# Nine weight blocks split straight out of PSUM, layer two's sums grown in their banks, and a new order of the steps

## Chip, cores and metric

The kernel runs on one core of one Trainium2 chip. The metric is the device time of one execution in microseconds (us), as the median of several runs. Engines are named as the profile names them: PE is TensorE (matmuls; PEld its weight loads), DVE is VectorE, ACT is ScalarE, POOL is GpSimd, SP is SyncE, which issues the DMAs here.

## What is computed

```python
def sm_attn(qq, kk, vv):                      # per batch and head
    a = softmax(scale * qq @ kk.T)
    return a @ vv
p_packed = sm_attn(p, k, v)                   # 32 packed rows for 576 of k, v
out = sm_attn(q, p_packed, p_packed)          # 8 batches, 8 heads, 576 x 64
x = out.transpose(0, 2, 1, 3).reshape(4608, 512)
h = maximum(maximum(x @ w1, x @ w2), x @ w3)  # 512 -> 768
result = h @ w_out                            # 768 -> 512
```

Everything is float32. x is never formed: the softmax of the second attention, a2, is multiplied by p_packed @ w. That product is what the kernel calls pw, and it is small: 256 rows (8 heads of 32) by 768 for each of three w.

## The kernel before

One pass handles one batch b of eight. Batches 0 and 1, the conversion of the weights and the first steps of batch 2 are written out as a list of steps, `START`; batches 2 to 7 go through a second list, `LOOP`, once each. A word of a list is a letter for a stage, its indices, and a suffix v, g or a that sends one instruction to DVE, POOL or ACT; each time that a word comes up, its stage goes on to its next `yield`. The lists alone set the order of the instructions on each engine. A steady pass on PE begins with the scores of the next batch (`S`, tile s). Then come layer one of its own batch (`N`, six blocks j of 128 hidden columns, tiles mi_j_a, b, c, d and f) and layer two (`O`, tiles mo_n_m for seven products n and two halves m). Between them lie the values (`V`, tile av) and queries (`Q`, tile s again) of the next batch, and six projections (`P`, tiles pw_j): 3, 4 and 5 of its own batch, 0, 1 and 2 of the next.

Layer one with b >= 2 is `layer_fast`: seven block products with sums instead of eight, all of them in three matmuls (hi by hi, lo by hi, hi by lo). Its weights are nine blocks of 128 x 128 for each j: six are blocks of pw, one is a sum of two, two are differences. Each is split in two parts, hi and lo. `project` first copies pw out of PSUM, scaled (`pf`, L508, ACT), then POOL makes the three sums (L514 to L516), then `part` casts three blocks at a time to hi on ACT (L470, in the helper L118) and subtracts for lo (L472, in the helper L123) on DVE or POOL. The tiles are `pt_j_0` to `pt_j_2`.

Layer two is `layer_out`: seven products, in the order 1, 5, 2, 6, 7, 4, 3, each with two halves m, each of nine matmuls into a bank of its own. `finish` joins them: DVE adds 6 to 1 (tile u), 7 to that (v), and subtracts 4 (tile s), and the results are stored from SP.

PSUM has two pools: `ps_big` with two buffers of two banks (s, av, most pw) and `ps_moe` with four single banks (mi, mo, and pw_0 and pw_3, each in two). A bank is reused when its last reader is done. In SBUF the tag "w" has six buffers, shared by the weights w loaded for a projection, by pf, e and u. A load of w (L171, on SP, letter m) therefore waits for the last reader of what stood in its buffer, and every later DMA on SP waits behind it.

Of the kernel before, what the change touches and what calls it, by code (L numbers as in the profile page):

```python
# [829 lines left out]
```

## Time and profile before

| what | value |
| --- | --- |
| time, median of 3 runs | 465.64 us (464.93 to 466.1) |
| the profiled execution, its own time | 463.21 us |
| its span, first to last instruction | 461.4 us |
| granted clock of PE, mean | 0.998 |
| PE busy | 449.3 us, 97% |
| DVE busy | 403.9 us, 88% |
| ACT busy | 287.8 us, 62% |
| POOL busy | 281.2 us, 61% |

The median and the profiled execution are different executions; the span leaves out what lies ahead of the first and behind the last instruction. Passes of LOOP are measured below from the first matmul of S of one pass to that of the next; the last has no S. Busy time of PE counts matmuls that overlap once.

### The profile page before, as it was taken

How to read it: one execution, taken by the hardware profiler on the slowest of the kernel's cores; microseconds unless marked ns; L12 is line 12 of the kernel's file. 1: busy time of each engine (PE TensorE's matmuls, PEld its weight loads, DVE VectorE, ACT ScalarE, POOL GpSimd, SP SyncE). 2: the span in 40 equal slices, each digit the busy share in tenths (PEclk: the TensorE clock that was granted, in tenths of full speed). 3: DMA queues.
4: the chain of work that ended last, by engine and by line, in shares of the span. 5: the costliest groups of instructions: out<-in, count | busy, mean ns of one | idle time of the engine just before them, and what ended most of it. 6: DMA issues, size and time to landing. Idle time of an engine off the chain costs nothing.

```text
span 461.4 us, 11887 instructions
## 1 busy us (share of the span) xinstructions
PE 449.3 (97%) x4592; PEld 387.9 (84%) x4592; DVE 403.9 (88%) x836; ACT 287.8 (62%) x614; POOL 281.2 (61%) x292
## 2 busy tenths in 40 slices
PE   8999999999999999999999999999999999999996
PEld 3467878889997888989799788988789887997996
DVE  2788999899988899999999899989989999897972
ACT  2587977475444857477664866657574776747740
POOL 0567786763577555765658655576457656587532
PEclk9999999999999999999999999999999999999999
DMA  8999873630438773198704794086721974034002
GB/s 294 402 378 390 295 245 116 233 141 0 164 113 324 222 293 121 37 345 280 278 26 138 301 344 132 26 294 214 300 107 42 370 248 164 27 114 169 1 7 97
DMA packets 31160, 89.89 MB, mean 195 GB/s; under 512 B 3072, under 2 KB 16384, under 8 KB 31104
## 3 DMA queue, kind: packets, MB, share of 16 engines
q1 hardware_dynamic: 31104, 89.14, 53.9%
q8 instruction: 36, 0.59, 0.5%
q14 instruction: 20, 0.16, 0.1%
HBM read 71.43 MB, written 17.69 MB: 193 GB/s over the span
## 4 chain that ended last, share of the span: by engine, by line
PE 77%; DMA 12%; DVE 6%; issue 2%; ACT 1%; SPq 1%; POOL 1%; DVEq 0%; POOLq 0%; ACTq 0%
PE mo L686 27%; PE mi_b L546 9%; PE mi_a L546 7%; PE mi L623 7%; PE pw L493 7%; DMA w<-wk 6%; PE mi_f L546 5%; PE mi_d L546 5%; PE mi_c L546 3%; DMA wk<-w 2%; DMA wi<-in_wi 2%; PE s L252 2%; PE s L366 2%; PE idle L131 1%; PE av L338 1%
## 5 line engine op out<-in xcount | busy, mean ns | idle before, releaser
L123 POOL TENSOR_TENSOR pt<-pf,pt 128x384 fp32r<-128x384 f32 x43 | 45.9, 1074 | 21.6 <-ACT pt L118 21.1
L118 ACT CAST pt<-pf 128x384 fp32r<-128x384 f32 x102 | 49.2, 516 | 5.3 <-PE mi_d L546 2.3
L657 POOL TENSOR_TENSOR r<-r 128x288 f32<-128x288 f32 (+1 forms) x35 | 37.6, 1075 | 23.4 <-DVE r L552 17.5
L546 PE MATMUL mi_b<-a2h,pt 128*128 128x288 f32 x216 | 48.4, 310 | 0.0
L546 PEld LDWEIGHTS mi_b<-a2h,pt 128*128 128x128 f32 x216 | 33.8, 188 | 17.2 <-DVE u L552 6.2
L546 PE MATMUL mi_a<-a2h,pt 128*128 128x288 f32 x216 | 47.1, 299 | 0.0
L493 PE MATMUL pw<-w,pt 64*32 64x384 f32 x768 | 40.4, 492 | 3.1 <-DMA w<-wk 2.0
L686 PE MATMUL mo<-ych,xl 128*128 128x288 f32 x144 | 42.5, 295 | 0.0
L686 PE MATMUL mo<-ych,xh 128*128 128x288 f32 x144 | 42.5, 295 | 0.0
L686 PE MATMUL mo<-ycl,xh 128*128 128x288 f32 x144 | 42.4, 295 | 0.0
L623 PE MATMUL mi<-a2h,ph 128*128 128x288 f32 x132 | 40.7, 308 | 0.1
L118 ACT COPY u<-mi_b 128x288 f32<-128x288 f32 x36 | 14.4, 401 | 40.9 <-PE mi_b L546 32.6
L623 PE MATMUL mi<-a2l,ph 128*128 128x288 f32 x132 | 39.0, 295 | 0.6 <-DVE a2l L123 0.6
L623 PE MATMUL mi<-a2h,pl 128*128 128x288 f32 x132 | 39.0, 295 | 0.0
L123 DVE TENSOR_TENSOR pt<-pf,pt 128x384 fp32r<-128x384 f32 x65 | 38.2, 594 | 0.8 <-ACT pt L118 0.6
L508 ACT ACTIVATE pf<-pw 128x384 f32<-128x384 f32 (+1 forms) x50 | 31.7, 648 | 11.1 <-PE pw L493 11.1
L207 POOL TENSOR_TENSOR w<-w,wi 128x512 int32<-128x512 int32 x18 | 23.7, 1330 | 23.9 <-ACT wi L192 18.1
L514 POOL TENSOR_TENSOR pf<-pf 128x128 f32<-128x128 f32 x36 | 18.7, 519 | 30.3 <-ACT pf L508 30.3
L546 PEld LDWEIGHTS mi_a<-a2h,pt 128*128 128x128 f32 x216 | 34.1, 188 | 0.1
L552 DVE TENSOR_TENSOR u<-mi_d,u 128x288 f32<-128x288 f32 x72 | 32.2, 448 | 1.2 <-ACT u L118 1.0
L515 POOL TENSOR_TENSOR pf<-pf 128x256 f32<-128x256 f32 x36 | 30.2, 839 | 2.8
L546 PE MATMUL mi_a<-a2l,pt 128*128 128x288 f32 x108 | 31.8, 294 | 0.0
(164 smaller groups left out, 1558.0 us busy)
## 6 DMA issues: line engine op xcount, KB each, us to landing
w<-wk SPq DMA_DIRECT2D x33, 768.0 KB, 6.9
kt<-in_kp SPq DMA_DIRECT2D x16, 640.0 KB, 6.9
wi<-in_wi SPq DMA_DIRECT2D x18, 512.0 KB, 8.3
v<-in_va SPq DMA_DIRECT2D x16, 512.0 KB, 9.0
q<-in_qt SPq DMA_DIRECT2D x14, 576.0 KB, 5.7
wk<-w SPq DMA_DIRECT2D x6, 768.0 KB, 7.3
xk<-x SPq DMA_DIRECT2D x6, 576.0 KB, 5.4
wi<-in_wo SPq DMA_DIRECT2D x6, 512.0 KB, 4.8
```

The source lines that it names most:

```text
L118: e.copy(out=out, in_=src)
L123: on(default).tensor_tensor(out=lo, in0=src, in1=hi.bitcast(F32), op=ALU.subtract)
L207: nc.gpsimd.tensor_tensor(out=dst.bitcast(I32), in0=dst.bitcast(I32), in1=up, op=ALU.add)
L493: nc.tensor.matmul(out=ps[r][NP * n:NP * n + NP, 0:NW * P], lhsT=pt_sb[b % 2][o, NP * n:NP * n + NP], rhs=w[o, n * NW * P:(n + 1) * NW * P ...
L508: nc.scalar.activation(out=full[:, r], in_=x, func=AF.Copy, scale=2.0 ** -WS)
L514: on("g").tensor_tensor(out=f[:, 6], in0=f[:, 1], in1=f[:, 4], op=ALU.add)
L515: on("g").tensor_tensor(out=f[:, 7:9], in0=f[:, 3:4].to_broadcast([P, 2, P]), in1=f[:, 4::2][:, 0:2], op=ALU.subtract)
L546: nc.tensor.matmul(out=out, lhsT=x, rhs=y, start=(start and k == 0 and n == 0), stop=(stop and k == len(terms) - 1 and n == 2), skip_group ...
L552: join = lambda out, x, y, op: nc.vector.tensor_tensor(out=out, in0=x, in1=y, op=op)
L623: nc.tensor.matmul(out=sums[b, j, hf, x][:, 0:HS], lhsT=w[:, r, x * P:(x + 1) * P], rhs=a[:, c], start=(r == 0 and n == 0), stop=(r == R - ...
L657: less = lambda out, x, y: on("g").tensor_tensor(out=out, in0=x, in1=y, op=ALU.subtract)
L686: nc.tensor.matmul(out=ps[:, 0:HS], lhsT=w[:, x, m * P:(m + 1) * P], rhs=h[:, z], start=(p == 0 and i == 0), stop=(p == NQ - 1 and i == 2),)
```

## The change

Three edits and two new lists.

1. `nine` takes the place of the copy, the sums on POOL and `part` for b >= 2. The block r = 1, i = 1 is copied out, scaled, by ACT (128 x 128). ACT casts hi of all six blocks straight from PSUM, and DVE forms lo from PSUM and hi. DVE makes the sums with `mix`, one operand in PSUM and one in SBUF, in three instructions. Then four blocks (three sums and one in the place of block 4) are split once more: 128 x 384 as tile ps, 128 x 128 in pt. The buffers change with it: pt (six blocks) has the tag "w", where pf stood; pf (six blocks) has "pl".
2. For b >= 2, products 6, 7 and 4 of layer two are added by PE into the bank of product 1 (`CHAIN`), after the join has read it. The joins of these three products become scaled copies (`join`, `scaled`) on ACT. The block of w_out for product 4 is negated once.
3. START, from its twelfth line on, and all of LOOP are in a new order.

The sums of batches 0 and 1 in layer two stay as they were.

```diff
@@ -53,34 +53,34 @@
...
-E110a N11 w61 N11 P03 E110 E111a H01g N11 N11 P03 N03 H00g P10 C60 C61 C60 H01g E051 P15 P00 C65 C64 E030a P12 N03
...
-m04 S1 N00 N00 N00a N00 N00a A10 N00 N00a N00 P02g N00 P02g N00a N00 N00 A10 N00 A11 N00a N00 N00 N00 N01 N00
...
+S1 A11 N00 N00 N00a N00 N00a N00 N00a m03 N00 N00 N00a N00 A11 N00 A10 A10 N00 N00a N00 N00 N00 N00 m04 N01 N01
...
@@ -229,6 +229,7 @@
         combine(t[:, 1], t[:, 0], x[:, 0], ALU.subtract)
         yield 0
         combine(x[:, 1], x[:, 0], x[:, 1], ALU.subtract)
+        nc.vector.tensor_scalar(out=x[:, 3], in0=x[:, 3], scalar1=-1.0, scalar2=None, op0=ALU.mult)
         yield 0
         yield from split(slice(0, 4), x)
         yield from split(slice(4, 6), t)
@@ -464,14 +465,46 @@
     def plain(b, j):
         return b == 0 and j in PLAIN
 
-    def part(b, j, f, k):
-
-        t = pool.tile([P, 2, 3, P], F32R, name=f"pt{b}_{j}_{k}", tag=("ph", "pl", "pl" if j % 2 else "ph")[k], bufs=3)
-        copy(t[:, 0], f[:, 3 * k:3 * k + 3])
-        yield 0
-        split_lo(t[:, 1], f[:, 3 * k:3 * k + 3], t[:, 0], "v")
+    def nine(b, j, ps, rows):
+
+        x = [y[:, 0:NW * P].rearrange("p (i x) -> p i x", x=P) for y in ps]
+        f = pool.tile([P, 6, P], F32, name=f"pf{b}_{j}", tag="pl", bufs=3)
+        copy_scaled(f[:, 0], x[1][:, 1])
+        yield 0
+        t = pool.tile([P, 2, R, NW * P], F32R, name=f"pt{b}_{j}", tag="w", bufs=NJ)
+        v = t.rearrange("p h r (i x) -> p h (r i) x", x=P)
+        for i in range(6):
+            pw[b, j, i] = v[:, 0, i], v[:, 1, i]
+        for r, y in rows:
+            nc.scalar.activation(out=t[:, 0, r], in_=y, func=AF.Copy, scale=2.0 ** -WS)
+            yield 0
+            nc.vector.scalar_tensor_tensor(
+                out=t[:, 1, r], in0=y, scalar=2.0 ** -WS, in1=t[:, 0, r].bitcast(F32), op0=ALU.mult, op1=ALU.subtract,
+            )
+            yield 0
+        mix = lambda out, a, c, op: nc.vector.scalar_tensor_tensor(
+            out=out, in0=a, scalar=2.0 ** -WS, in1=c, op0=ALU.mult, op1=op,
+        )
+        mix(f[:, 1], x[0][:, 1], f[:, 0], ALU.add)
+        mix(f[:, 2:4], x[1][:, 0:1].to_broadcast([P, 2, P]), f[:, 0:2], ALU.subtract)
+        mix(f[:, 4], x[0][:, 0], f[:, 3], ALU.add)
+        yield 0
+        q = pool.tile([P, 2, 3, P], F32R, name=f"ps{b}_{j}", tag="ph", bufs=3)
         for i in range(3):
-            pw[b, j, 3 * k + i] = t[:, 0, i], t[:, 1, i]
+            pw[b, j, 6 + i] = q[:, 0, i], q[:, 1, i]
+        copy(q[:, 0], f[:, 1:4])
+        yield 0
+        split_lo(q[:, 1], f[:, 1:4], q[:, 0])
+        yield 0
+        copy(v[:, 0, 4], f[:, 4])
+        yield 0
+        split_lo(v[:, 1, 4], f[:, 4], v[:, 0, 4])
+
+    def copy_scaled(out, x):
+        if on("a") is nc.scalar:
+            nc.scalar.activation(out=out, in_=x, func=AF.Copy, scale=2.0 ** -WS)
+        else:
+            nc.vector.tensor_scalar(out=out, in0=x, scalar1=2.0 ** -WS, scalar2=None, op0=ALU.mult)
...
         yield 1
-        if plain(b, j) or fast(b, j):
-            if fast(b, j):
-                f = wide(f"pf{b}_{j}")[:, 0:9 * P].rearrange("p (a x) -> p a x", x=P)
-                full = f[:, 0:6].rearrange("p (r a) x -> p r (a x)", r=R)
-            else:
-                full = pw[b, j] = pool.tile([P, R, NW * P], F32, name=f"pf{b}_{j}", tag="ph", bufs=3)
+        if fast(b, j):
+            yield from nine(b, j, ps, list(zip(parts, src)))
+            return
...
-            if plain(b, j):
-                return
-            on("g").tensor_tensor(out=f[:, 6], in0=f[:, 1], in1=f[:, 4], op=ALU.add)
-            on("g").tensor_tensor(out=f[:, 7:9], in0=f[:, 3:4].to_broadcast([P, 2, P]), in1=f[:, 4::2][:, 0:2], op=ALU.subtract)
-            on("g").tensor_tensor(out=f[:, 4], in0=f[:, 8], in1=f[:, 0], op=ALU.add)
-            yield 0
-            yield from part(b, j, f, 0)
-            yield 0
-            yield from part(b, j, f, 2)
-            yield 0
-            yield from part(b, j, f, 1)
             return
...
@@ -678,16 +699,25 @@
 
         for n, m in ORDER:
             x, y, z = PRODUCTS[n]
-            ps = sums[b, n, m] = ps_moe.tile([P, 512], F32, name=f"mo{b}_{n}_{m}", tag="moe")
+            chain = b >= 2 and n in CHAIN
+            if chain:
+                sums[b, n, m] = sums[b, 1, m]
+            else:
+                sums[b, n, m] = ps_moe.tile([P, 512], F32, name=f"mo{b}_{n}_{m}", tag="moe")
+            ps = sums[b, n, m]
+            assert not chain or (b, CHAIN[n], m) in read
             for p in range(NQ):
                 w_hi, w_lo = x_op[p]
                 h_hi, h_lo = hid[b, p, y]
                 for i, (w, h) in enumerate(((w_hi, h_hi), (w_lo, h_hi), (w_hi, h_lo))):
                     nc.tensor.matmul(
                         out=ps[:, 0:HS], lhsT=w[:, x, m * P:(m + 1) * P], rhs=h[:, z],
-                        start=(p == 0 and i == 0), stop=(p == NQ - 1 and i == 2),
+                        start=(not chain and p == 0 and i == 0), stop=(p == NQ - 1 and i == 2),
+                        skip_group_check=True,
                     )
             yield 0
+
+    CHAIN, read = {6: 1, 7: 6, 4: 7}, set()
...
@@ -699,12 +729,18 @@
             return tiles[name]
 
         def scaled(out, n, m):
-            nc.scalar.activation(out=out, in_=sums[b, n, m][:, 0:HS], func=AF.Copy, scale=2.0 ** -WS)
+            copy_scaled(out, sums[b, n, m][:, 0:HS])
 
         def add(out, n, m, x, scale=2.0 ** -WS):
             nc.vector.scalar_tensor_tensor(
                 out=out, in0=sums[b, n, m][:, 0:HS], scalar=scale, in1=x, op0=ALU.mult, op1=ALU.add,
             )
+
+        def join(out, n, m, x):
+            if b >= 2:
+                scaled(out, n, m)
+            else:
+                add(out, n, m, x)
...
         for n, m in ORDER:
+            read.add((b, n, m))
...
             elif n == 6:
-                add(temp("u")[:, m], n, m, temp("s")[:, m])
+                join(temp("u")[:, m], n, m, temp("s")[:, m])
             elif n == 7:
-                add(temp("v")[:, m], n, m, temp("u")[:, m])
...
             elif n == 4:
-                add(temp("s")[:, m], n, m, temp("v")[:, m], -2.0 ** -WS)
+                join(temp("s")[:, m], n, m, temp("v")[:, m])
```

**First place: the projections 3, 4 and 5 on PE, and their loads on SP.** In the kernel before, PE meets pw_4 in the middle of layer one's second block (mi_1); the rows are those of the pass of batch 3, and a2h, a2l and pt are the split operands.

```order
L546 MATMUL mi_1_d<-a2l_1_0_2882,pt_1_0_2806 128x288
L546 MATMUL mi_1_a<-a2h_1_0_2860,pt_1_2_2884 128x288 x2
L546 MATMUL mi_1_a<-a2l_1_0_2882,pt_1_2_2884 128x288
L493 MATMUL pw_4_3028<-w_4_2899,pt_75 32x384 x8
L546 MATMUL mi_1_b<-a2h_1_1_2852,pt_1_1_2896 128x288 x2
L546 MATMUL mi_1_b<-a2l_1_1_2857,pt_1_1_2896 128x288
L546 MATMUL mi_1_f<-a2h_0_1_2727,pt_1_0_2806 128x288 x2
```

pw_3 follows after the end of mi_1 and pw_5 after mi_2, each between matmuls of layer one. In the changed kernel the same place of the same batch reads:

```order
L526 MATMUL pw_3_0_3055<-w_3_2945,pt_75 32x384
L526 MATMUL pw_3_1_3056<-w_3_2945,pt_75 32x384
L526 MATMUL pw_4_3077<-w_4_2982,pt_75 32x384 x8
L526 MATMUL pw_5_3095<-w_5_2997,pt_75 32x384 x8
L567 MATMUL mi_2_b<-a2h_0_1_2803,pt_2_2756 128x288 x2
L567 MATMUL mi_2_b<-a2l_0_1_2847,pt_2_2756 128x288
L567 MATMUL mi_2_b<-a2h_1_1_2805,pt_2_2756 128x288 x2
L567 MATMUL mi_2_b<-a2l_1_1_2833,pt_2_2756 128x288
```

The three projections now stand next to each other, between mi_1 and mi_2. Their weights are loaded on SP, behind the stores of the pass before; this is SP in the kernel before, with the engines or DMA queues on which each transfer waits:

```order
L715 DMA out_t<-u_2808 128x2x288 [waits DMAHW5_49,DVE_49]
L171 DMA w_4_2899<-wk_1516 128x1536 [waits PE_49]
L171 DMA w_3_2996<-wk_1811 128x1536 [waits DMAHW7_49,DVE_49]
L171 DMA w_5_2998<-wk_1309 128x1536 [waits DMAHW0_49,DVE_49]
L157 DMA v_3039<-in_va 128x1024 [waits DMAHW1_49]
L158 DMA v_3039<-in_vb 64x256 [waits DMAHW2_49]
```

And after:

```order
L751 DMA out_t<-u_2784 128x2x288 [waits DMAHW5_49,DVE_49]
L171 DMA w_3_2945<-wk_1462 128x1536 [waits DMAHW6_49]
L171 DMA w_4_2982<-wk_2020 128x1536 [waits Pool_49]
L171 DMA w_5_2997<-wk_1225 128x1536 [waits DMAHW1_49,DMAHW0_49,DVE_49]
L157 DMA v_3047<-in_va 128x1024
L158 DMA v_3047<-in_vb 64x256 [waits DMAHW2_49]
```

pw_3 was second and is first; w_5 stays last of the three and waits for DVE as before, w_4 waits for POOL where it waited for PE. The places of the three on SP, behind the stores and ahead of the loads of v, are unchanged.

**Second place: DVE and ACT in layer two.** DVE in the kernel before, around the end of layer one's last block (mi_5) and the start of mo, in the same pass (z and e belong to the second softmax of the next batch, r, yb and yc to layer two's operands):

```order
L552 TENSOR_TENSOR u_5_3422<-mi_5_a,u_5_3422 128x288 [waits DVE_49,PE_49]
L412 RECIPROCAL z_4_0_0_3463<-z_4_0_0_3463 128x18 [waits Activation_49]
L552 TENSOR_TENSOR u_5_3422<-mi_5_d,u_5_3422 128x288 [waits PE_49]
L552 TENSOR_TENSOR r_2_3293<-u_5_3422 128x576 [waits DVE_49]
L414 TENSOR_TENSOR e_0_3356<-e_0_3356,z_4_0_0_3463 128x576
L405 TENSOR_REDUCE z_4_1_0_3534<-e_1_3365 128x18 [waits Pool_49]
L123 TENSOR_TENSOR ybl_2_3536<-r_2_3293,ybh_2_3527 128x576 [waits Activation_49]
L417 STREAM_TRANSPOSE e_0_3356<-e_0_3356 128x576 [waits DVE_49]
L412 RECIPROCAL z_4_1_0_3534<-z_4_1_0_3534 128x18 [waits Activation_49]
L657 TENSOR_TENSOR r_2_3293<-r_2_3293 128x2x288 [waits DVE_49,Pool_49]
L123 TENSOR_TENSOR ycl_1_3548<-r_1_3085,ych_1_3546 128x864 [waits Activation_49]
L123 TENSOR_TENSOR ycl_2_3562<-r_2_3293,ych_2_3550 128x864 [waits Activation_49]
```

And after:

```order
L573 TENSOR_TENSOR u_5_3386<-mi_5_a,u_5_3386 128x288 [waits DVE_49,PE_49]
L573 TENSOR_TENSOR u_5_3386<-mi_5_d,u_5_3386 128x288 [waits PE_49,Activation_49]
L406 TENSOR_REDUCE z_4_0_0_3461<-e_0_3392 128x18 [waits Activation_49]
L481 SCALAR_TENSOR_TENSOR pt_0_3463<-pw_0_0_3448,pt_0_3463 128x384 [waits PE_49,Activation_49]
L481 SCALAR_TENSOR_TENSOR pt_0_3463<-pw_0_1_3449,pt_0_3463 128x384 [waits PE_49,Activation_49]
L573 TENSOR_TENSOR r_2_3247<-u_5_3386 128x576 [waits DVE_49]
L485 SCALAR_TENSOR_TENSOR pf_0_3459<-pw_0_0_3448,pf_0_3459 128x128
L485 SCALAR_TENSOR_TENSOR pf_0_3459<-pw_0_1_3449,pf_0_3459 128x256 [waits DVE_49]
L485 SCALAR_TENSOR_TENSOR pf_0_3459<-pw_0_0_3448,pf_0_3459 128x128 [waits DVE_49]
L678 TENSOR_TENSOR r_1_3108<-r_1_3108 128x2x288
L123 TENSOR_TENSOR ybl_2_3523<-r_2_3247,ybh_2_3504 128x576 [waits Activation_49]
L413 RECIPROCAL z_4_0_0_3461<-z_4_0_0_3461 128x18
```

Between mi_5's last joins and layer two's operands there now stand the two lo of pw_0 and three sums with an operand in PSUM; PE's mo_5_0 takes the bank of pw_0_1, whose last reader is the second sum (128x256). On ACT, between the reading of products 1 and 4 (u, v and s are tiles of the result), before:

```order
L702 ACTIVATE t_3579<-mo_5_0_3517 128x288 [waits PE_49]
L702 ACTIVATE t_3579<-mo_5_1_3552 128x288 [waits PE_49]
L508 ACTIVATE pf_1_3593<-pw_1_3483 128x768 [waits DMAHW7_49,DMAHW5_49,DMAHW0_49]
L118 CAST pt_0_0_3595<-pf_0_3494 128x384 [waits Activation_49]
L118 CAST pt_1_0_3644<-pf_1_3593 128x384 [waits Activation_49]
L118 CAST pt_0_2_3683<-pf_0_3494 128x384 [waits Pool_49]
L118 CAST pt_0_1_3687<-pf_0_3494 128x384 [waits Pool_49]
L118 CAST a2h_1_1_3690<-e_1_3365 128x576 [waits DVE_49]
L118 CAST a2h_1_0_3698<-e_1_3365 128x576 [waits DVE_49]
```

And after:

```order
L505 ACTIVATE u_3612<-mo_1_0_3479 128x288 [waits PE_49]
L118 CAST ps_0_3626<-pf_0_3459 128x384
L505 ACTIVATE u_3612<-mo_1_1_3494 128x288 [waits PE_49]
L118 CAST a2h_0_1_3631<-e_0_3392 128x576 [waits DVE_49]
L118 CAST a2h_1_1_3633<-e_1_3412 128x576 [waits DVE_49]
L505 ACTIVATE v_3635<-mo_1_0_3479 128x288 [waits PE_49]
L505 ACTIVATE v_3635<-mo_1_1_3494 128x288 [waits PE_49]
L118 CAST ps_1_3669<-pf_1_3577 128x384 [waits DVE_49]
L118 CAST a2h_1_0_3673<-e_1_3412 128x576 [waits Activation_49,Pool_49]
L118 CAST a2h_0_0_3688<-e_0_3392 128x576 [waits DVE_49]
```

The copies of the grown banks (u, v, s) now stand in ACT's queue between the casts of a2h, which wait for DVE's transposes of e.

## Rows read from the trace of the kernel before

**Rows 1.** The page, its first part: busy time, share and instructions of each engine
```profile
PE 449.3 (97%) x4592; PEld 387.9 (84%) x4592; DVE 403.9 (88%) x836; ACT 287.8 (62%) x614; POOL 281.2 (61%) x292
```

**Rows 2.** Windows of the six passes of LOOP: length; busy of PE, PEld, DVE, ACT, POOL
```profile
140.84:194.79 53.95, 53.53 (x573) 47.45 (x580) 48.64 (x101) 35.55 (x79) 32.94 (x37) 1.00 0.56 201
194.79:247.78 52.99, 52.99 (x566) 46.74 (x566) 49.67 (x103) 35.60 (x79) 33.72 (x38) 1.00 0.57 205
247.78:301.10 53.32, 53.14 (x566) 46.90 (x565) 49.66 (x103) 35.60 (x79) 33.78 (x38) 1.00 0.57 203
301.10:356.03 54.93, 53.29 (x566) 46.97 (x566) 49.97 (x103) 35.46 (x79) 33.74 (x38) 1.00 0.55 198
356.03:410.20 54.17, 53.60 (x568) 47.34 (x568) 49.88 (x103) 35.44 (x79) 33.78 (x38) 1.00 0.50 176
410.20:457.80 47.60, 46.70 (x373) 43.52 (x371) 36.00 (x63) 25.05 (x56) 26.91 (x29) 1.00 0.22 78
```

**Rows 3.** Timeline of PE around one projection alone: start, duration, what
```profile
263.78 0.42 PE L546 MATMUL mi_d<-a2h,pt 128*128 128x288 f32 x2
264.04 0.29 PE L546 MATMUL mi_d<-a2l,pt 128*128 128x288 f32 x1
264.26 0.88 PE L493 MATMUL pw<-w,pt 64*32 64x384 f32 x16
265.07 0.53 PE L546 MATMUL mi_b<-a2h,pt 128*128 128x288 f32 x2
265.44 0.29 PE L546 MATMUL mi_b<-a2l,pt 128*128 128x288 f32 x1
```

**Rows 4.** Timeline of PE around a pair of projections
```profile
229.19 0.29 PE L546 MATMUL mi_d<-a2l,pt 128*128 128x288 f32 x1
229.41 1.52 PE L493 MATMUL pw<-w,pt 64*32 64x384 f32 x32
230.87 0.40 PE L686 MATMUL mo<-yah,xh 128*128 128x288 f32 x1
231.11 0.29 PE L686 MATMUL mo<-yah,xl 128*128 128x288 f32 x1
```

**Rows 5.** Timeline of PE, one wait: idle time and what ended it in brackets
```profile
140.84 1.32 PE L252 MATMUL s<-kt 64*32 64x288 f32 x32 [0.84 <-DMA kt<-in_kp]
```

**Rows 6.** View of the tile w: issue to landing of its 33 loads
```profile
DMA to landing us min/median/max: 4.3/6.9/9.7
```

**Rows 7.** The chain that ended last: start, duration, what
```profile
278.07 4.54 DMA w<-wk
```

**Rows 8.** Groups by form of DVE from 140.8 us on: count, busy us, mean ns
```profile
L123 DVE TENSOR_TENSOR pt<-pf,pt 128x384 fp32r<-128x384 f32 x62 | 35.4, 578 | 0.7 <-ACT pt L118 0.4
L552 DVE TENSOR_TENSOR u<-mi_d,u 128x288 f32<-128x288 f32 x72 | 32.2, 448 | 1.2 <-ACT u L118 1.0
L552 DVE TENSOR_TENSOR r<-u 128x576 f32<-128x576 f32 x36 | 29.3, 815 | 0.5
L123 DVE TENSOR_TENSOR a2l<-e,a2h 128x576 fp32r<-128x576 f32 x22 | 23.8, 1106 | 0.0
L123 DVE TENSOR_TENSOR ycl<-r,ych 128x864 fp32r<-128x864 f32 x18 | 19.8, 1123 | 0.0
L123 DVE TENSOR_TENSOR ybl<-r,ybh 128x576 fp32r<-128x576 f32 x12 | 9.1, 755 | 0.7 <-ACT ybh L118 0.7
L311 DVE STREAM_TRANSPOSE x<-a 128x128 f32<-128x128 f32 x20 | 4.6, 272 | 0.0
L447 DVE TENSOR_TENSOR e<-e 128x288 f32<-128x288 f32 x5 | 2.2, 447 | 0.0
```

**Rows 9.** Groups by line of DVE, whole span: an operand in PSUM
```profile
L530 DVE SCALAR_TENSOR_TENSOR pl<-pw,ph 128x768 fp32r<-128x768 f32 x11 | 10.5, 951 | 2.6 <-ACT ph L528 2.5
```

**Rows 10.** Groups by form of ACT from 140.8 us on
```profile
L118 ACT CAST a2h<-e 128x576 fp32r<-128x576 f32 x20 | 13.5, 675 | 13.0 <-DVE e L447 7.2 <-DVE e L417 5.6
L702 ACT ACTIVATE s<-mo 128x288 f32<-128x288 f32 x12 | 4.8, 412 | 5.6 <-PE mo L686 5.6
```

More of the change, by code (lines that the diff above doesn't have):

```diff
@@ new lines @@
+B20 B20 E130 B20v O0 P00 H14v W0g E131a N15 N13 N13 D0v H03g D4v O0 P20 B21 P21 O0 E151 H14a B21 F0a W2g E131 W0a
+E131 H03a H12g H05v H03v H11g H10v P20a F0a H14g D0 B20 P20 F0 F0 O0 B20 P20 P20 B20a H15a O0 D1 F0 P20 O1 P20 B20
+B21v B21 O1 F1a O1 H15v H15v O1 B20v H11g H13a F1a B21 B21a O0 P21a W0g H11g F1a F0 B21 H13v O0 H13v H15g B21v F0
+P20a O0 F0 k31 F1v H13g B21 P21 H11a O0 B20 F0 P20v H11v H15a O1 P22 H13a F1 H15v H13g O0 F0 O1 O0 O1 O1 F0 F0 P22v
+O1 P22 O1 O1 B20a B21a F1 T2g P22 F0 P21 F0 B21v P20a F1 T2g T2g F1 P20v F1 F1 O1 P22 F1 B20v D4 T2a F1 F1 T2g P22g
@@ new lines @@
+N02a N02 q11 N02 P05 P05 N02a N02 N02 P03a N02 N02a k20 N02 P04a N02 H01g N02 N02 N03 N03 N03a N03 N03a P05 H01g
+N03 P03g P04g N02 Z10 N03a N03 P04a N03 N03a N03 P04g q10 N03 N03 H02g P05a N03v N03 N03 N03 H01a N04 H02a N03
+N04 N04a N04 N04a N04 H02v N03 H01v V101 V101 N04a H03a N04 N04 N04a N04 m12 K1 N04 N04 N04a K1v N04 N04 N04 Q1
+N05 N04 N05 N04 P05g P05a N05a N05 B10 H04v N05a N05 H03g m10 N05a B10 P05v N05 B11 N05 H04a N05a N05 N05 N05
+N05a H03g k21 B11 N05 N05 B10g H04g N05 N05 B11g P10 B10 P10a B10 P10 P12 P10 P10 B10v P10 N05 O0 F0a P10 O0
@@ L84 @@
+H05a H03v m11 B11 F0a H03a O0 H05v H05g O0 F0a B10 P11 H05v H03v O0 H05a O0 B11 H05v P11a F0a B11a P12a B11 P12
+B10v F0 B10 F0 O0 P11 O0 F0a B11g O0 B11 P12 P10a P11 T1g F0a B10a B11a F0a O0 P11 T1g F0a O0 F0 B11v F0 P12 T1v
+P11a P10v P10v T1a B10v O0 T1v T1a F0a O0 F0a T1g P10g P12a P12g P11g P12a P12g P11a O0 F0 F0 P11g
 """
@@ L499, in project @@
         yield 1
-        if plain(b, j) or fast(b, j):
-            if fast(b, j):
-                f = wide(f"pf{b}_{j}")[:, 0:9 * P].rearrange("p (a x) -> p a x", x=P)
-                full = f[:, 0:6].rearrange("p (r a) x -> p r (a x)", r=R)
-            else:
-                full = pw[b, j] = pool.tile([P, R, NW * P], F32, name=f"pf{b}_{j}", tag="ph", bufs=3)
+        if fast(b, j):
+            yield from nine(b, j, ps, list(zip(parts, src)))
+            return
+        if plain(b, j):
+            full = pw[b, j] = pool.tile([P, R, NW * P], F32, name=f"pf{b}_{j}", tag="ph", bufs=3)
             for r, x in zip(parts, src):
@@ L726, in finish @@
             elif n == 6:
-                add(temp("u")[:, m], n, m, temp("s")[:, m])
+                join(temp("u")[:, m], n, m, temp("s")[:, m])
             elif n == 7:
-                add(temp("v")[:, m], n, m, temp("u")[:, m])
+                join(temp("v")[:, m], n, m, temp("u")[:, m])
                 if m == 1:
```

32 lines of the change are left out of this document (10 added, 22 removed).

## Prediction

> **What bounds the kernel now.** The first view is the first part of the page [rows 1]: PE is busy 97% of the span, DVE 88%, ACT and POOL near 62%. A mean over the span doesn't tell what ends a stage, so the second view cuts LOOP into its six passes [rows 2]. In the second pass PE is busy 52.99 of 52.99 us. In the others it isn't quite: 53.95, 53.32, 54.93 and 54.17 us long. A pass is thus 52.99 us of PE's own sequence plus waits, and DVE (49.7 us in it), ACT (35.6) and POOL (33.8) all have slack. Work taken from them is worth nothing by itself; what counts is how PE's sequence is laid out, and what makes PE wait.
>
> The third view is PE's timeline around the projections. Plain matmuls start 0.13 us apart (two in 0.26 from 263.78 to 264.04; I take 0.133). A projection stands out: from the matmul ahead of it at 264.04 to the one at 265.44 it takes 1.40 us, of which three are plain matmuls (one ahead, two behind), 0.40; so one alone costs 1.00 [rows 3]. Two side by side take 1.92 from 229.19 to 231.11, less two plain matmuls, 1.65 [rows 4]. The second costs 0.65: 0.35 of every stretch of projections is the price of going to the small tiles (64*32) and back.
>
> **The change, part by part.**
>
> *Fewer stretches of projections.* A pass of before has four alone and one pair: 4 x 1.00 + 1.65 = 5.65 us. After the change 3, 4 and 5 are one stretch of three, 0 and 2 a pair, and 1 stands alone inside layer two: 1.00 + 2 x 0.65 = 2.30, 1.65 and 1.00, together 4.95. That saves 0.70 in each of five passes. The last pass has only 3, 4 and 5: three alone, 3.00, become 2.30, again 0.70. Six times 0.70 is **4.2 us**; START has one stretch fewer, **0.3**. No other row tells of a third projection beside two; that it costs 0.65 like the second is an estimate, 0.65 to 1.00 its bounds, so the term lies between 2.1 and 4.2 for LOOP. The rows of the second lie in the same sort of tile, so I take 4.2. PE's undisturbed pass becomes 52.3 us.
>
> *The nine blocks, on DVE.* Counted per pass. Removed: 11 subtractions of 384 columns at 0.578, 6.4 us; one a2l, 1.11; five instructions on 576 columns that go to POOL, near 0.76 each, 3.8; eight of 288 columns (the six joins among them) at 0.45, 3.6 [rows 8]. That is 14.9. Added: 4 lo of 768 columns at 0.95 [rows 9], 3.8; 4 lo of 384, 0.55 each between the 0.45 of 288 and the 0.95 of 768, 2.2; 12 sums of 128 columns at 0.27, 3.3; 6 of 256, 0.41 each between 128 and 288, 2.5; one subtraction of 384 and three small ones, 1.4 [rows 8]. That is 13.2. DVE goes from 49.7 to some 48 us of a 52.3 us pass; instructions side by side overlap a little, so up to 49. It stays below PE, with less room than its 94% of before leaves by 0 to 1 us. ACT gains six copies of 0.41 [rows 10] and loses casts (17 of 384 columns become five, and five of 128); POOL loses 18 sums and gains five of DVE's. Both stay far from the bound: nothing.
>
> The sums and lo read PSUM. Rows of the same operation and size don't differ: 448 ns with an operand in PSUM (u<-mi_d), 447 from SBUF (e<-e) [rows 8]. So I price by size alone. [...]
>
> *Layer two in its banks.* PE's matmuls are the same number. A product that adds to a bank must wait until the copy of the sum so far has been read, but product n, half m comes nine matmuls (1.2 us) after the bank's last write, against one copy of 0.41 [rows 10]: hidden, if ACT is free. Price if it is not: the second rival.
>
> *The stalls of before.* The windows over 52.99 sum to 0.96 + 0.33 + 1.94 + 1.18 = 4.4 us; the last pass has 47.60 - 46.70 = 0.9 without PE [rows 2]; ahead of LOOP, PE waits 0.84 for kt [rows 5]. Together 6.1. The loads and joins that they hang on all move, so I count them as gone, and count new ones.
>
> *The new stalls.* Three places. (a) w_5 waits on SP for DVE's last reader of its buffer, layer one's first join r<-u, some 7.0 us after S began (S 1.3 [rows 5], 33 matmuls of mi_0 4.4, the last joins 0.45 and 0.82 [rows 8]). Alone in flight it takes 4.3 to 4.5 us [rows 6, 7] and lands at 11.3 to 11.5. PE reaches pw_5 after S, 66 matmuls and two projections: 1.3 + 8.8 + 1.3 = 11.4. It may be 0.1 early; with the handovers between the engines I take it as up to 0.4 late. (b) mo_5_0 needs the bank of pw_0_1. From the end of pw_0 PE has pw_2 and 18 matmuls, 0.76 + 2.4 = 3.15 us, to run. DVE can begin lo after ACT's copy and first hi (about 0.7) and then has two lo, r<-u and two sums: 2 x 0.55 + 0.82 + 0.27 + 0.41 = 2.6. Sum 3.3: late by some 0.2. (c) mi_2's banks c and d are freed by DVE's sums of pw_3, near 0.1. I take 0.6 per pass for five, 1.0 for the last with its loads, 0.6 for START: **4.6**, a net gain of **1.5** on stalls.
>
> *Sum.* 463.21 - 4.2 - 0.3 - 1.5 = 457.2 for an execution like the profiled one. The median lies 2.43 above it (465.64), so 459.6.
>
> **The rivals.**
>
> *No stalls left.* The margins in (a) to (c) are tenths, and a little in PE's favour would clear them. Then all 6.1 come back: 465.64 - 4.5 - 6.1 = 455.0. For it: pass two of before had none. Against: three places at or beyond zero.
>
> *w_5 lands late.* It is the last of three loads; those of before took 6.9 in the median [rows 6]. If w_4, behind POOL, is still in flight, w_5 takes 5.6 rather than 4.5: 1.1 in each of six passes eats the 6.0, and the time is 465.6, the same. At 6.9 it would be 2.4 times six, 474. Against: it leaves only at 7.0, when w_3 and w_4 have had time to land, and a load that the chain shows behind such a wait took 4.54 [rows 7].
>
> *DVE late in layer two (slower).* ACT's queue is in order: the copies v, which mo_4_0 waits for, stand behind two casts a2h, and these behind DVE's transposes of e. From the sums of pw_0 to the second transpose DVE has 13 instructions: two ycl at 1.12, seven of 576 columns at 0.76, two of 288 at 0.45, two small at 0.27 [rows 8], 9.0 us; then a2h 0.68 and v 0.41 [rows 10], 10.1. PE goes from mo_5_0 to mo_4_0 in 72 matmuls and pw_1, 9.6 + 1.0 = 10.6. The margin is 0.5, less the handovers. If DVE comes 2 us late (an operand of POOL late, z or e*z), PE loses some 1.7 in five passes, 8.5: 468. It decides from 1.5 us: 1.2 x 5 is the 6.0 gained. For it: DVE has hardly any slack. Against: it has a little more than before.
>
> *The stretches don't pay.* If the third projection cost 1.00, the gain would be 2.1 less: 461.7, still faster.
>
> **How the numbers follow.** The forecast with its own spread (0.1 to 1.0 of stalls per pass, the third projection between its bounds) is 456.5 to 463, chance 0.62; no stalls left 0.12; w_5 late, with about the old time, 0.12; DVE late 0.14. What a measurement of this kernel tells from no change is about 0.3%, 1.4 us: 464.2 to 467.0. The forecast and the first rival are faster; of w_5 late most is same, a part slower; DVE late is slower in most of it, and a small start of it faster or same. Faster 0.76, same 0.11, slower 0.13. The range goes from the first rival's 455.0, a little under it, to the old time: 454.5 to 466.
>
> **What would show it.** Right: PE's timeline has one stretch of 48 matmuls of pw in some 2.2 us between mi_1 and mi_2; passes near 52.3 plus 0.5; PE's waits named w (pw_5) and DVE's sums (mo_5_0, mi_2); DVE near 48 us a pass. Wrong: waits of PE of over 1 us a pass at pw_5 on the load, or at mo_4 on ACT's copy; DVE's instructions on PSUM longer than their sizes say; or a new stall in START, where the order is new from its twelfth line and I worked out only a few margins.

## The result, and the profile after

The changed kernel takes 467.9 us in the median of 20 runs (464.09 to 474.24), the kernel before, run beside it, 464.54 (461.88 to 466.31). The ratio is 1.0056, with a 95% interval of 1.0029 to 1.0083: slower by half a per cent, where 1.3% faster was forecast. The ratio leaves out the four slowest runs of the changed kernel (471.35 to 474.24 us) as slow runs, while the medians are over all 20. The profiled execution took 468.16 us, its span went from 461.4 to 466.4.

The first part of the page, to compare with [rows 1]:

```profile
PE 447.6 (96%) x4592; PEld 388.5 (83%) x4592; DVE 396.7 (85%) x868; ACT 279.3 (60%) x639; POOL 262.2 (56%) x250
```

PE, DVE, ACT and POOL are all busy for less time than before, and the span is longer: the added time is nearly all time in which PE waits. The windows of LOOP's six passes, with the columns of [rows 2]:

```profile
140.77:195.22 54.45, 52.84 (x566) 46.95 (x565) 48.05 (x108) 34.14 (x83) 32.50 (x33) 1.00 0.60 205
195.22:250.35 55.13, 52.77 (x566) 46.90 (x565) 49.27 (x109) 33.97 (x83) 30.49 (x31) 1.00 0.58 197
250.35:303.57 53.22, 52.84 (x566) 46.96 (x565) 48.89 (x109) 34.08 (x83) 30.65 (x31) 1.00 0.59 204
303.57:361.05 57.48, 54.22 (x566) 48.33 (x565) 49.01 (x109) 34.08 (x83) 30.43 (x31) 0.97 0.56 189
361.05:415.90 54.85, 52.62 (x567) 46.89 (x567) 48.73 (x109) 33.96 (x83) 30.41 (x31) 1.00 0.52 173
415.90:463.20 47.30, 45.94 (x374) 43.65 (x372) 30.54 (x59) 24.61 (x59) 23.40 (x25) 1.00 0.23 82
```

LOOP starts where it did (140.77 and 140.84). Its passes differ by up to 4.3 us, though PE has the same matmuls in each: the third is 53.22 us, the fourth 57.48. DVE is busy for 48 to 49 us of a pass, as forecast. What PE waits for says the view of PE's waits: total, times, longest.

```profile
PE pw L526 <- DMA w<-wk: 7.7, 4, 3.2
PE s L367 <- DMA q<-in_qt: 2.7, 3, 1.2
```

The longest wait, in the fourth pass, on PE's timeline:

```profile
313.67 1.52 PE L526 MATMUL pw<-w,pt 64*32 64x384 f32 x32
318.37 0.88 PE L526 MATMUL pw<-w,pt 64*32 64x384 f32 x16 [3.18 <-DMA w<-wk]
319.18 0.85 PE L567 MATMUL mi_b<-a2h,pt 128*128 128x288 f32 x2
319.83 0.44 PE L567 MATMUL mi_b<-a2l,pt 128*128 128x288 f32 x1
```

pw_3 and pw_4 run at 313.67. pw_5 waits 3.18 us for its weights. The matmuls behind it then start 0.24 us apart rather than 0.13, until 322.5. The windows around that, whose third number from the end is the granted clock, show why:

```profile
313.67:318.37 4.70, 1.52 (x33) 0.48 (x32) 4.26 (x10) 1.92 (x5) 3.50 (x5) 1.00 0.99 366
319.18:322.40 3.22, 3.22 (x21) 3.22 (x14) 0.10 (x1) 0.98 (x3) 1.96 (x2) 0.50 0.11 44
322.60:325.00 2.40, 2.40 (x20) 2.40 (x19) 1.80 (x4) 1.89 (x6) 0.46 (x1) 1.00 0.55 148
```

The clock was granted at 0.50 for 3.4 us (319.15 to 322.57) after PE had stood idle for 3.18; that cost about 1.5 us more: from the start of pw_5 to that of the 15th matmul behind this projection it takes 4.3 us, in the second pass 2.8.

SP's timeline of that pass (S at 303.57), and then the loads that the chain of waits names, with the time from issue to landing:

```profile
305.17 0.37 SPq L751 DMA_DIRECT2D out_t<-u  x1
305.59 5.51 SPq L171 DMA_DIRECT2D w<-wk  x3
311.14 0.43 SPq L157 DMA_DIRECT2D v<-in_va  x1
314.58 0.67 SPq L315 DMA_DIRECT2D xk<-x  x1
```

```profile
202.43 5.41 DMA w<-wk
216.20 8.66 DMA q<-in_qt
310.78 7.55 DMA w<-wk
368.26 6.53 DMA w<-wk
422.15 5.71 DMA w<-wk
```

SP stands at the third load of w for over 4 us. That load, w_5, leaves at 310.78, 7.2 us into the pass (forecast 7.0), and takes 7.55 us (forecast 4.3 to 4.5). v, x and, behind x, q leave after it. In the first and third pass the same load left at 7.2 too and took 4.1 and 4.2 us.

### The profile page after: what moved, and what is told of

It reads as the page before. It is cut to its first block, busy times and chain, and to the rows that moved or that the text cites. A ratio compares the mean times of both kernels' runs of the same rounds, so it can differ in the third digit from the quotient of the medians.

```text
span 466.4 us, 11887 instructions
## 1 busy us (share of the span) xinstructions
PE 447.6 (96%) x4592; PEld 388.5 (83%) x4592; DVE 396.7 (85%) x868; ACT 279.3 (60%) x639; POOL 262.2 (56%) x250
## 4 chain that ended last, share of the span: by engine, by line
PE 80%; DMA 10%; DVE 7%; issue 1%; ACT 0%; POOL 0%; SPq 0%; DVEq 0%; POOLq 0%
PE mo L713 29%; PE mi L644 9%; PE mi_b L567 8%; PE mi_a L567 7%; PE pw L526 5%; DMA w<-wk 5%; DMA q<-in_qt 5%; PE mi_f L567 5%; PE mi_d L567 4%; PE idle L131 3%; PE mi_c L567 3%; PE s L367 2%; PE s L253 2%; DVE r L658 1%; DVE u L573 1%
## 5 line engine op out<-in xcount | busy, mean ns | idle before, releaser
L678 POOL TENSOR_TENSOR r<-r 128x288 f32<-128x288 f32 (+1 forms) x43 | 42.2, 982 | 38.2 <-DVE r L573 28.9
L481 DVE SCALAR_TENSOR_TENSOR pt<-pw,pt 128x384 fp32r<-128x384 f32 (+1 forms) x48 | 34.5, 747 | 4.4 <-ACT pt L479 4.3
L485 DVE SCALAR_TENSOR_TENSOR pf<-pw,pf 128x128 f32<-128x128 f32 (+1 forms) x108 | 35.8, 332 | 2.5
L567 PE MATMUL mi_b<-a2l,pt 128*128 128x288 f32 x108 | 32.1, 297 | 0.0
L123 POOL TENSOR_TENSOR ps<-pf,ps 128x384 fp32r<-128x384 f32 x30 | 30.3, 1017 | 2.5 <-ACT ps L118 2.0
L567 PE MATMUL mi_a<-a2h,pt 128*128 128x288 f32 x144 | 31.0, 297 | 0.0
L479 ACT ACTIVATE pt<-pw 128x384 fp32r<-128x384 f32 (+1 forms) x48 | 29.6, 658 | 2.2 <-DVE pf L507 1.9
L567 PE MATMUL mi_f<-a2h,pt 128*128 128x288 f32 x144 | 30.3, 299 | 0.0
L644 PEld LDWEIGHTS mi<-a2h,ph 128*128 128x128 f32 x132 | 24.8, 188 | 6.5 <-issue 2.3
L401 POOL TENSOR_TENSOR e<-e,m 128x576 f32<-128x576 f32 (+1 forms) x15 | 15.9, 1070 | 24.2 <-DVE m L399 24.1
```

What stands on the lines that cost most here:

```text
L123: on(default).tensor_tensor(out=lo, in0=src, in1=hi.bitcast(F32), op=ALU.subtract)
L401: on("g").tensor_tensor(out=e3, in0=e3, in1=m.unsqueeze(2).to_broadcast([P, nt, NP]), op=ALU.subtract)
L479: nc.scalar.activation(out=t[:, 0, r], in_=y, func=AF.Copy, scale=2.0 ** -WS)
L481: nc.vector.scalar_tensor_tensor(out=t[:, 1, r], in0=y, scalar=2.0 ** -WS, in1=t[:, 0, r].bitcast(F32), op0=ALU.mult, op1=ALU.subtract,)
L485: mix = lambda out, a, c, op: nc.vector.scalar_tensor_tensor(out=out, in0=a, scalar=2.0 ** -WS, in1=c, op0=ALU.mult, op1=op,)
L567: nc.tensor.matmul(out=out, lhsT=x, rhs=y, start=(start and k == 0 and n == 0), stop=(stop and k == len(terms) - 1 and n == 2), skip_group ...
```

## The experiments

Each kernel was run beside the kernel before on the same chip; ratios are to that, with a 95% interval. Between runs, compare ratios rather than times: the kernel before took 461.9 to 464.5 us beside them. Lists are shown by the words that move: m05 is the load of w_5 for the pass's own batch and m13 that of w_3 for the next, v, k and q are loads of v, kt and q, and X1 stores x and loads it again as xt. "S+7" is 7 us after the first matmul of S of its pass.

**Is it the load of w_5 at all?** Run h3 leaves the load out, f1 lets it leave earlier, e1 moves PE's need for it, and f2 does as f1 and moves the need as well.

*Without the load* (run h3):

```diff
 def load_m(b, j):
+    if b >= 2 and j == 5:
+        loaded["m", b, j] = loaded["m", b, 4]
+        return
     loaded["m", b, j] = wide(f"w{b}_{j}")
```

> The changed kernel without the loads of w_5 in LOOP: projection 5 reads the tile of w_4 instead, so that its result is not the reference's. One transfer of 768 KB per pass, its buffer and SP's wait for it are gone; PE's matmuls and all else stay. Theory A: PE waits for no w at the three projections, not for q, and the clock holds: near the forecast, 456 to 459, with only the small waits for DVE at mi_2 and mo_5. Theory B (PE would wait elsewhere for as long): 463 or more.

Measured: 456.52 us, ratio 0.9868 (0.9810 to 0.9926). PE waits for one w, 0.3 us, and for no q; five passes of 52.66 to 52.99 us:

```profile
141.65:194.35 52.70, 52.62 (x566) 46.90 (x565) 47.54 (x108) 34.08 (x83) 32.41 (x33) 1.00 0.58 197
194.35:247.34 52.99, 52.91 (x567) 46.96 (x566) 48.66 (x109) 34.04 (x83) 30.67 (x31) 1.00 0.54 190
300.09:352.85 52.76, 52.68 (x566) 46.96 (x565) 48.61 (x109) 34.05 (x83) 30.67 (x31) 1.00 0.56 191
```

The loss hangs on this load, with its buffer and its place in SP's queue, which are gone here too: the pass is the forecast's 52.3 of PE's own plus 0.4 to 0.7.

*w_5 in another buffer* (run f1), by asking for it ahead of u_1:

```diff
-m04 N01 N01 N01a m05
+m04 m05 N01 N01 N01a
```

> The changed kernel with the load of w_5 asked for ahead of tile u_1, so that it takes the buffer of pt_0 (free when PE ends mi_0, 5.9 us into the pass) and not that of u_0 (free after DVE's join, 7.0). Theory A (the loss is the late issue of w_5, and x and q queued behind it on SP): w_5 leaves 1.1 us earlier, PE's waits for w fall from 7.7 to some 3.5 us, those for q from 2.7 to under 1, the slow clock behind the longest wait mostly goes: 4 to 7 us less than the changed kernel. Theory B (transfers are slow by themselves, whenever they leave): under 2 us less.

Measured: 460.54 us (459.90 to 461.52, a spread of 1.6 where the changed kernel's was 10), 0.9964 (0.9935 to 0.9992). w_5 leaves at S+5.4. The waits, and ACT where the new one comes from:

```profile
PE mi_a L567 <- ACT mi_b L118: 2.7, 6, 0.7
PE pw L526 <- DMA w<-wk: 0.8, 1, 0.8
```

```profile
255.93 0.40 ACT L118 COPY u<-mi_b 128x288 f32<-128x288 f32 x1 [1.31 <-DVE r L573]
```

One buffer was free at S+5.4, one at S+7.2. Now u_1 gets the later, ACT's first copy into it waits for DVE's join r, and PE's next matmul starts 0.55 us late in a pass (0.4 of it idle; once 0.7), 2.7 us of idle time in all. The waits for q are gone, as expected.

*w_5 early, and projection 5 inside mi_2* (run f2; `-P05 P03g v11 N02 P04 N02` becomes `+P03g v11 N02 P04 N02 P05`, beside the edit of f1):

> As the run before, and projection 5 stands between the second and the third product of mi_2, nine matmuls (1.2 us) later, so that the sums of pw_3 keep their cover. Theory A: PE's waits for w under 1 us, none for q, no slow clock; six stretches of projections more than the changed kernel, 2.1 us: some 8 to 10 us less than the changed kernel, below the kernel before by 3 to 5. Theory B: a wait comes up in its place (mi_2 on DVE, mo on ACT), no gain on the kernel before.

Measured: 460.85 us, 0.9971 (0.9946 to 0.9997). On PE's timeline the stretch of two costs 1.65 and the one alone 1.00, as forecast; the waits for w go from 0.8 to 0.2, and u_1's wait stays: no gain of 8 to 10.

*Projection 5 after mi_2* (run e1), moved with the four steps behind it:

> The changed kernel with projection 5 alone after mi_2, as it stood before, 4.6 us later in the pass; all else as in the changed kernel. [...] Theory B (the loss lies in DVE, ACT or PSUM in layers one and two, and the wait for w only stands where another would): PE waits elsewhere for the same time, about 470.

Measured: 475.43 us, 1.0288 (1.0237 to 1.0339). Were the wait for w_5 the whole loss, an estimated 461 would come: 467.9, less 7.7 of waits for w and 1.5 of the slow clock, plus 6 x 0.35 for the stretch that stands alone again. No wait for w or q is left, but others came, from where I put the steps:

```profile
PE mi_d L567 <- DVE u L573: 9.0, 6, 1.6
PE mi_c L567 <- DVE pf L485: 4.1, 6, 0.7
```

DVE stood 2.9 us a pass at pw_5's lo, behind which mi_3's joins waited. The miss says how little room there is on the other engines' queues, and nothing against the load.

**Why does w_5 take 4 us here and 7 there?** First the suspect that follows it, v (run e2):

```diff
-m04 N01 N01 N01a m05 ... v10 ... v11
+m04 v10 v11 N01 N01 N01a m05
```

> The changed kernel with the two loads of v issued ahead of w_5 instead of behind it, so that they use the 4 us in which SP waits for w_5's buffer. Theory A1 (w_5 is slowed by the v loads that share the DMA engines with it, and the loads of x and q are held up behind both): PE's waits for w fall from 7.7 to 2 to 4 us and those for q from 2.7 to under 1, 462 to 465. Theory A2 (the issue of w_5 at 7 us alone is too late): waits for w stay above 6, those for q fall, 465 to 467. Theory B (loads don't matter): 468.

Measured: 483.34 us, 1.0464 (1.0413 to 1.0514), PE's waits for w 20.6 us. With v ahead of it w_5 still left at S+7.2 and took 6.9 to 8.9 us, one of them 8.2:

```profile
DMA to landing us min/median/max: 8.2/8.2/8.2
```

Neither form of the theory had that: what is issued ahead of a transfer can make it late, here 1 to 4 us ahead. Then v behind x instead (run i1; `X1 v10 v11` at the third X1):

> The changed kernel with the loads of v moved behind x and xt on SP, so that nothing is issued within some 3 us behind w_5; its issue at 7 us stays. If the v transfers behind it are what makes w_5 slow: it takes 4.1 to 4.5 us in every pass, PE's waits for w fall from 8 to under 2, those for q too since x no longer queues behind v; 459 to 462, if v itself is in time for av. If w_4 and w_3 ahead of it, still in flight, are: w_5 takes 5 to 6.5 us in some passes as before, waits for w of 4 us or more, 463 to 467.

Measured: 468.94 us, 1.0132 (1.0062 to 1.0201). With nothing but x behind it w_5 took 4.1, 7.0, 4.9, 7.2 and 7.0 us: v behind it is not the cause. But in the 20 passes of four runs (the changed kernel twice, e1 and i1) there is a pattern. Where w_4 landed up to 1.2 us after w_5's issue, w_5 took 4.1 to 4.2 us (six passes); where w_4 landed 1.5 to 2.8 us after, 4.9 to 7.6 (fourteen). So w_3 was sent ahead, from the pass before (run i3; for the first pass, from the end of START):

```diff
-S1 A11 N00 N00 N00a N00 N00a N00 N00a m03
+S1 A11 N00 N00 N00a N00 N00a N00 N00a
...
-F0a O0 F0 B11v
+F0a m13 O0 F0 B11v
```

> The changed kernel with the load of w_3 asked for in the pass before, ahead of its last three stores on SP, so that at the start of a pass only w_4 leaves, and is down before w_5 leaves at 7.2 us. If w_3 and w_4 still in flight are what makes w_5 slow: it takes 4.1 to 4.3 us in every pass and lands at 11.3 to 11.5, PE's waits for w fall from 8 us to under 1, and with u_1 in the buffer of pt_0 there is no wait for ACT at mi_1: 457 to 460. If not: w_5 takes 5 to 7 us in some passes, 463 to 468.

Measured: 460.91 us (458.31 to 465.33), 0.9938 (0.9910 to 0.9967). SP now reads (S at 195.95, w_3 for that pass left at 188.16), and w_5's landing in the fourth pass of the profile:

```profile
188.16 0.41 SPq L171 DMA_DIRECT2D w<-wk  x1
193.32 0.39 SPq L751 DMA_DIRECT2D out_t<-t  x1
197.97 5.53 SPq L171 DMA_DIRECT2D w<-wk  x2
```

```profile
DMA to landing us min/median/max: 4.2/4.2/4.2
```

w_4 lands by S+6.4 to 8.2, and w_5, leaving at 7.2 as before, takes 4.1 to 4.3 in these five passes. So the loads sent just ahead of w_5 made it late; only w_3 was moved, so what w_4 does alone is not shown. PE's waits for w are 0.2. One of the twelve executions still took 465.33 us with a mean clock of 0.993, so a long wait may still come up now and then. The buffer of pt_0 on top (run i4):

> As i3, and w_5 in the buffer of pt_0 as in f1. w_5 lands near 10 us, 1.4 ahead of its need; the wait of 0.55 us for ACT's copy into u_1 comes back in each of six passes: 459 to 461, that is some 2 us more than i3 if i3's w_5 is in time, and less than i3 if it is not.

Measured: 460.40 us (459.97 to 461.95), 0.9927 (0.9899 to 0.9956): u_1's 2.7 us are back, q's waits are gone, the sum is the same. v behind x with the edit of f1 (run i2) adds as little:

> The kernel with w_5 in the buffer of pt_0 and with the loads of v moved behind x and xt. w_5 is in time without it in five of six passes, so by the theory of its lateness little is left to gain: within 1 us of the run with the buffer of pt_0 alone, and the wait of 0.55 us for ACT's copy into u_1 in each pass stays.

Measured: 460.07 us, 0.9948 (0.9921 to 0.9974), as expected.

**The waits for q.** The second load of q stood behind kt; `k20` was put behind `q10` (run e3):

> The changed kernel with the load of kt that stands between the two loads of q moved behind both. Theory A (kt's 640 KB ahead of the second q make it late): PE's waits for q fall from 2.7 us to under 0.7, the rest stays, about 466. Rival (q is late since x and xt ahead of it on SP are): waits for q fall by less than 1, about 467.5.

Measured: 466.81 us (460.94 to 469.36), 1.0058 (1.0016 to 1.0100). In its profile PE waits for no q, and 9.0 us for w, no less than before: no net gain can be seen while w_5 is late. On i3, where it isn't (run j1):

> i3 with the load of kt moved behind both loads of q, as in e3. Left in i3 are PE's waits for q, 2.6 us, and some 0.4 of DVE's per pass. If q is late only because kt's 640 KB stand ahead of the second q: waits for q under 0.5, 458 to 459 and a narrower spread. If the first q and x, held up on SP behind w_5 until 7.2, are late themselves: waits for q or for xt stay above 1.5, 460 to 461.

Measured: 459.89 us, 0.9921 (0.9893 to 0.9950): no wait for q, 1.3 for one w. And with v behind x as well (run j2):

> As j1, with the loads of v behind x and xt as well, so that x leaves some 3 us earlier. If x and xt are what holds q up: no wait for q or xt, 457.5 to 459. If v, 3 us later, becomes late for av, a wait for v comes up instead, 460 or more.

Measured: **456.67 us** (456.42 to 457.99), 0.9859 (0.9822 to 0.9896). This version beats both kernels; PE's waits and two of its passes:

```profile
PE pw L526 <- DMA w<-wk: 0.4, 1, 0.4
PE s L367 <- DMA q<-in_qt: 0.3, 1, 0.3
```

```profile
247.94:300.76 52.82, 52.70 (x566) 46.84 (x565) 48.61 (x109) 34.07 (x83) 30.61 (x31) 1.00 0.61 205
300.76:353.58 52.82, 52.74 (x566) 46.85 (x565) 48.64 (x109) 33.97 (x83) 30.61 (x31) 1.00 0.60 205
```

**The stretches, alone.** The kernel before with projection 4 beside 3 was tried in three placements of the steps behind it (runs e4, f3 and h4, in this order):

```diff
-N01 P04 N01a ... P04a ... P03 P03a
+N01 N01a ... P03 P04 P03a
```

> The kernel before with projection 4 moved next to projection 3, behind mi_1: one stretch fewer in each of six passes, no other part of the change. By the term of the prediction each is worth 0.35 us: 6 x 0.35 = 2.1, about 462.4 against 464.5. Rival (a stretch of projections costs the same wherever it stands, or its place only moves a wait): 464.5.

> The kernel before with projection 4 next to 3, as in the run before of this name, but POOL's sums for block 4 stand behind those of block 3, so that ACT's queue doesn't wait there for POOL. If the stretches are worth 0.35 us each: no wait of 1.7 us at mi_2, 2.1 us less than the kernel before. If they are not: the same time as before.

> The kernel before with projection 4 next to 3, now with POOL's sums for block 4 behind all of POOL's work for block 3. In the run before of this kind a wait of 0.58 us for POOL at mi_3 ate the gain. If that was all: 2 us less than the kernel before; if the gain turns into yet another wait, the same time.

Measured: 468.00 us, 1.0131 (1.0084 to 1.0178); 463.25, 1.0020 (0.9987 to 1.0053); 464.55, 1.0034 (1.0005 to 1.0063). On PE a pair at that place takes 1.65 to 1.75 us, as in [rows 4], so that 0.25 to 0.35 is saved. Each time a queue behind it lost as much or more:

```profile
PE mi_a L546 <- ACT u L118: 9.2, 6, 1.6
```

```profile
PE mi_b L546 <- POOL pt L123: 2.5, 6, 0.4
```

```profile
PE mi_a L546 <- ACT mi_b L118: 5.4, 6, 0.9
```

So the 2.1 us were not had in the old splitting of the blocks by these three; whether some placement would was not settled.

**The chain, alone and left out.** The second edit of the change on the kernel before, and the kernel of f1 without it, its joins on DVE again (runs f4 and h1; the diff is that of h1):

```diff
-chain = b >= 2 and n in CHAIN
+chain = False
```

> The kernel before with the second edit alone: products 6, 7 and 4 of layer two grow in the bank of product 1, the joins are scaled copies on ACT, the lists are those of before except that products 7 and 4 and their reading come in an order in which each bank is read first. Prediction's view (PE's matmuls are the same number, a copy of 0.41 us is hidden by nine matmuls, DVE loses 2.7 us of a pass that it has slack for): within 1 us of the kernel before. Rival (ACT's queue holds the copies up): PE waits at mo_7 or mo_4 by 0.5 to 2 us per pass, 3 to 10 us slower.

> The kernel with w_5 in the buffer of pt_0, without the second edit: products 6, 7 and 4 of layer two have banks of their own again and DVE joins them. DVE gets 6 x 0.45 = 2.7 us more per pass, from 49 to 51.6 of a pass of some 53.4; ACT loses six copies. Prediction's view (work off PE's path costs nothing until it reaches PE's 52.3): within 1.5 us of the run with the chain. Rival (DVE is close enough to the bound that waits on it grow): slower by 3 us or more, with PE waiting for DVE in layer two and at S.

Measured: 480.37 us, 1.0375 (1.0303 to 1.0447), and 483.11, 1.0447 (1.0387 to 1.0506). In the first PE waits 6.5 us for ACT's copies t and 5.1 for w. In the second:

```profile
PE mi_b L567 <- DVE s L735: 16.3, 5, 4.2
```

DVE's join of product 4 stands in the new list behind splits and sums, and the bank that mi_0 needs comes free up to 4.2 us late; after each of these five waits the granted clock was 0.50 for 3.4 us (its mean over the execution 0.982). Neither run shows what the edit is worth: each puts it in a list written for the other case. They show that the edit and the list can't be judged apart; my view that it costs next to nothing either way missed by 18 and 22 us.

**The changed kernel again** (run h2), beside the runs h1, h3 and h4:

> The changed kernel itself once more, on the same chip as the other runs of this call. Theory A (the transfers of w_5 set its time, and how long one takes changes from execution to execution): PE's waits for w and q of 5 to 12 us in the profile, times spread over several us, 464 to 472. If it comes out under 462, the loss was not of the kernel.

Measured: 467.17 us (462.42 to 470.38), 1.0099 (1.0058 to 1.0141), with waits for w of 8.1 us.

## Why the prediction was wrong

**The stretches (4.2 us): right.** In a pass without a wait, PE's timeline after:

```profile
260.23 0.29 PE L567 MATMUL mi_d<-a2l,ps 128*128 128x288 f32 x1
260.45 2.21 PE L526 MATMUL pw<-w,pt 64*32 64x384 f32 x48
262.59 0.53 PE L567 MATMUL mi_b<-a2h,pt 128*128 128x288 f32 x2
262.96 0.29 PE L567 MATMUL mi_b<-a2l,pt 128*128 128x288 f32 x1
```

From 260.23 to 262.96 it is 2.73 us, less three plain matmuls 2.33, against 2.30; two are 1.65 and one 1.00 as before. PE's own pass is 52.3 us: the third pass, 53.22, has some 0.9 us of waits (0.4 for q, 0.3 and 0.2 in steps (b) and (c) below).

**The nine blocks and the chain, on DVE and ACT: right in size.** The sums cost 286 and 424 ns, lo 553 and 941, where 0.27, 0.41, 0.55 and 0.95 us were taken; DVE has 48 to 49 us per pass:

```profile
L485 DVE SCALAR_TENSOR_TENSOR pf<-pw,pf 128x128 f32<-128x128 f32 x66 | 18.8, 286 | 1.1
L485 DVE SCALAR_TENSOR_TENSOR pf<-pw,pf 128x256 f32<-128x256 f32 x33 | 14.0, 424 | 1.1
L481 DVE SCALAR_TENSOR_TENSOR pt<-pw,pt 128x384 fp32r<-128x384 f32 x22 | 11.2, 553 | 3.6 <-ACT pt L479 3.6
L481 DVE SCALAR_TENSOR_TENSOR pt<-pw,pt 128x768 fp32r<-128x768 f32 x22 | 20.3, 941 | 0.9 <-ACT pt L479 0.8
```

PE waits for ACT's copies of the grown banks nowhere in LOOP. The instructions on PSUM were within 16 ns of the prices taken by size. That rows of the same operation and size don't differ held for the pair it was read from, 448 and 447 ns, and not for all: 128 x 576 took 755 ns as ybl and 1106 as a2l [rows 8].

**Step (b), the bank of pw_0_1: right.** mo_5_0 starts 0.36 us behind the matmul ahead of it (287.75 to 288.11 in the third pass), 0.23 more than a plain one, and the next 0.07; 0.2 was forecast. The second sum and ACT's cast ybh end there within 0.05 us of each other, so which of the two PE waited for is not shown. **Step (c)** 0.15 to 0.18, against 0.1.

**Step (a), w_5: this failed.** The place and the issue were right (S+7.2 against 7.0) and so was the need (S+11.4). The size was not: "alone in flight it takes 4.3 to 4.5" held in two passes of five. w_4 is still landing, because w_3 and w_4 leave at S+2 and S+2.5, behind the last store, and then w_5 takes 5.4 to 7.6. The load that the 4.5 was read from [rows 7] left 6.9 us behind the one ahead of it on SP, w_5 leaves 4.7 behind w_4. The second rival had this mechanism, w_4 in flight, and I gave it 0.12, with the words that w_4 "have had time to land". I had the rows to doubt it: of the loads of before, half took 6.9 us or more [rows 6].

The root is in the first edit: pt, six blocks that live until their block of layer one is done, took the buffers where pf had stood, which was free after its last split. Of the six buffers with tag "w" none is then free for w_5 before S+5.4.

**What was left out of the sum.** Two things follow from w_5 that I gave no term. SP sends its loads in the order of the list (in the fourth pass w_5 left at 310.78, v at 311.14, x at 314.58, q at 324.44), so v, x and q left behind it, and PE waited 2.7 us for q. And after the longest wait the granted clock was 0.50, 1.5 us. The six passes of after hold 15.0 us of waits over PE's own time (322.1 from the first S to the last matmul, less 307.1, that is 316.6 of before, less its 5.3 of waits, less 4.2). Of these 7.7 are w, 2.7 q, 1.5 the clock, and 3.1 the rest. For LOOP I had 4.0 in all, with up to 0.4 a pass for w_5 in it; that leaves 1.6 for what measured 3.1. In the runs, what was issued ahead of w_5 set its time (6.9 to 8.9 us with v ahead, e2; 4.1 to 4.3 with w_3 sent earlier, i3), and what came behind did not (still 4.1 to 7.2 with v moved away, i1).

**START:** 0.5 us less was forecast to the start of LOOP, 0.07 came. Nothing was run on that.

Without the load of w_5 the kernel takes 456.5 us, 0.987 of the kernel before. The forecast, 459.6 of 465.64, is 0.987 too. That they agree is in part luck: in the profile of h3 the time from LOOP's first S to the last matmul is 6.8 us shorter than before, where 5.5 was forecast, as no pass waits for w_5 at all, and LOOP starts 0.8 us later (141.65), where 0.5 earlier was forecast.

## What to carry to other kernels

When a change gives a longer life to a tile in a shared pool, list for each load that uses the pool when its buffer comes free, what is still in flight then, and what stands behind it in the same queue; a load with no slack is not a term of tenths. When executions of a kernel spread more than before, look for a transfer that lands just when it is needed: here the spread went from 10 us to 1.6 when that load left 1.8 us earlier. An order of steps and the edit that it was written for are one thing: neither half, put into the other kernel, told what the whole is worth.
